# A DiT attention block: turning all four token tiles before the K projection

## The chip, the cores and the metric

The kernel runs on one core of one Trainium2 chip. The metric is the device time of one execution in microseconds (us). The engines are PE (TensorE, with PEld for its weight loads), DVE (VectorE), ACT (ScalarE), POOL (GpSimd) and SP (SyncE, which here only issues transfers).

## What is computed

The reference, cut to the path (x is 2 x 256 x 1152 in bf16, D = 1152; the weights are bf16):

```
mod = (silu(c) @ w_mod).reshape(B, 6, 1, D)
shift_a, scale_a, gate_a = mod[:, 0], mod[:, 1], mod[:, 2]
h = layernorm(x) * (1 + scale_a) + shift_a
q, k, v = split(h @ wqkv, 3)
p = softmax(einsum('bqd,bkd->bqk', q, k) * D ** -0.5)
out = x + gate_a * (einsum('bqk,bkd->bqd', p, v) @ wo)
```

## The kernel before

The 512 tokens (two batches of 256) are four tiles of 128 tokens, t = 0 to 3; tiles 0 and 1 are batch 0. D is nine blocks of 128, k = 0 to 8. Products with weights want the tokens along the free side, so each token tile is centred (its mean taken off, in `xc`), turned block by block on PE (`transposes`, line 249, into PSUM tiles `tp`), copied to `xcT` (line 256), and scaled by 1 + scale_a into `hTs` (lines 309 to 317). The division by the standard deviation is left for later: the deviations are made in `parts_sq` by POOL, turned on PE (`pT3`, line 467), masked, spread over partitions by a matmul with ones (`bc_ps`), and multiplied in afterwards.

**Means.** Tile 0 takes its mean from BN statistics on DVE. Tiles 1 and 2 take theirs from an ACT pass that sums the whole tile (`act_mean`, line 235). Tile 3 is summed by ACT and DVE together, 640 and 512 columns (lines 401 to 405). Variances come later, from `act_var` (ACT) for tiles 1 and 2, and from BN statistics for tile 3.

**Scale.** scale_a = silu(c) @ w_mod is computed in four parts, PA = blocks 0 and 1, PB = 2 to 4, PC = 5 and 6, PD = 7 and 8. For PA, PC and PD the weights are the stationary operand and the result lies along partitions (`scale_rows`, 32 columns a matmul; PA's bank is first filled with ones by `scale_open`, line 273, so its sums already hold the 1). PB uses four 32-column tiles of the array side by side (`scale_tiles`, line 297); its result is turned by DVE (`scale_turned`), which also adds the 1.

**K.** K's transpose is the sum over nine rows k of wK block (k, f) times hTs row k, f = 0 to 8. Five f are accumulated in five PSUM banks (`accs`); the other four are parked: their first two rows go through `psE` banks to `held` in SBUF (`pair`, `pair_part`, `park`, lines 327 to 343), the rest is added later (`held_block`, `add_held`). Rows 0 and 1 are done in three shares of the tokens: batch 0, tile 2, tile 3 (`k_part`, line 322, and the calls at 395 to 425). Tile 3 is summed, centred and turned between them. From row 2 on, a row is one matmul of 512 columns for each f (`k_step`, line 345).

**What sets the order.** Each engine's instructions run in the order in which the code calls them: the recorders (line 76) keep a list for each engine and `pin` (line 98) turns it into dependencies. The profile puts every one of them at line 85, so instructions are told apart by their tiles. Loads run on SP's queue in the order of lines 167 to 192: tiles 0, 1 and 2 of x (tile 2 in two pieces), scale part PA in two pieces, wK row 0, tile 3 of x, wK row 1, scale part PB, wK rows 2 to 4, and so on. PSUM is eight banks: five in a pool MM that goes round, and BA, BB and BC by name. PE starts with eleven filler matmuls on a constant.

Of the kernel before, what the change touches and what calls it, by code (L numbers as in the profile page):

```python
# [7 lines left out]
ACT = mybir.ActivationFunctionType  # L8
ALU = mybir.AluOpType
# [7 lines left out]
def kernel(  # L17
# [10 lines left out]
    P = 128  # L28
# [37 lines left out]
    def bank(shape, name, dtype=None, where=None):  # L66
        if where is None:
            where = ring[turn_no[0] % len(ring)]
            turn_no[0] += 1
        return where[0].tile(shape, dtype or F32, tag=where[1], name=name)  # L70
# [36 lines left out]
    def tok(b):  # L107
        return slice(b * N, (b + 1) * N)

    def one(t):  # L110
        return slice(t * P, (t + 1) * P)
# [22 lines left out]

    c_sb = const.tile([P, B, KT], BF16)
    x_sb = act.tile([P, TT, D], BF16)
    ones_row = const.tile([1, 2 * NR], BF16)
    gps.memset(ones_row, 1.0)
    sca.preload_act_table_set("natural_log_exp_and_others")
    sca.dma_start(out=c_sb, in_=c.rearrange("b (p k) -> p b k", k=KT))  # L140
# [7 lines left out]
    def load_x(t):  # L148
        spq.dma_start(out=x_sb[:, t, :], in_=x_f[t * P : (t + 1) * P, :])
# [4 lines left out]
    def load_s(part, k0, k1):  # L154
        load_mod(wS, 1, k0, k1, part[0] * P, part[1] * P)
# [13 lines left out]
    XS = 104  # L169
    spq.dma_start(out=x_sb[:XS, 2, :], in_=x_f[2 * P : 2 * P + XS, :])  # L170
    spq.dma_start(out=x_sb[XS:, 2, :], in_=x_f[2 * P + XS : 3 * P, :])
    load_s(PA, 0, 4)
    load_s(PA, 4, KT)
    load_k(0, 1)
    load_x(3)
    load_k(1, 2)
    load_s(PB, 0, 4)
    load_s(PB, 4, KT)
# [40 lines left out]
    nmean = const.tile([P, TT], F32)  # L219
    xc = act.tile([P, TT, D], BF16, tag="a1")  # L220
    xcT = act.tile([P, KT, T], BF16, tag="a2")
    ssum3 = small.tile([P, 1], F32, tag="ssum", name="ssum")

    def bn_part(t, st, s):
        vec.bn_stats(out=st[:, s, :], in_=x_sb[:, t, s * CW : (s + 1) * CW])
# [9 lines left out]
    def act_mean(t):  # L235
        sca.activation(out=xc[:, t, :], in_=x_sb[:, t, :], func=ACT.Copy, scale=-1.0 / D,
                       accum_out=nmean[:, t : t + 1])
# [5 lines left out]
    def centre(t, scalar, op, c0=0, c1=D):  # L243
        vec.tensor_scalar(out=xc[:, t, c0:c1], in0=x_sb[:, t, c0:c1], scalar1=scalar, scalar2=None, op0=op)

    HALF = ((0, 4), (4, KT))
    tps = {}

    def transposes(t, h, where):
        k0, k1 = HALF[h]  # L250
        tp = bank([P, 5, P], "tp", BF16, where)
        for k in range(k0, k1):
            ten.transpose(tp[:, k - k0, :], xc[:, t, k * P : (k + 1) * P], ident)
        tps[t, h] = tp

    def xcT_copy(t, h, on_dve, skip=0):
        k0, k1 = HALF[h]
        dst, srct = xcT[:, k0 + skip : k1, one(t)], tps[t, h][:, skip : k1 - k0, :]
        if on_dve:
            vec.tensor_copy(out=dst, in_=srct)  # L260
        else:
            sca.copy(out=dst, in_=srct)

    s1p = const.tile([P, KT, B], F32)
    hTs = act.tile([P, KT, T], BF16, tag="a3")
# [7 lines left out]
    def scale_open(part, where):  # L273
        n = part[1] - part[0]
        psS[part] = bank([P, n, NR], "psS", where=where)
        ten.matmul(psS[part].rearrange("p j r -> p (j r)"), lhsT=junk[0:1, :P], rhs=ones_row[0:1, 0 : n * NR],
                   start=True, stop=False, skip_group_check=True)
# [16 lines left out]
    wS_v = wS.rearrange("p kk (k j c) -> p kk k j c", k=KT, j=4)  # L294
    sT = const.tile([P, KT, 32], F32)

    def scale_tiles(part, where):
        psS[part] = bank([P, part[1] - part[0], 32], "psS", where=where)
        for kk in range(KT):
            for j in range(4):  # L300
                ten.matmul(psS[part][32 * j : 32 * j + 32], lhsT=sc_rhs(kk), rhs=wS_v[:, kk, part[0] : part[1], j, :],
                           start=(kk == 0), stop=(kk == KT - 1))

    def scale_turned(part):
        vec.transpose(out=sT[:, part[0] : part[1], :].rearrange("p k c -> p (k c)"),
                      in_=psS[part].rearrange("p k c -> p (k c)"))
        vec.tensor_scalar_add(out=s1p[:, part[0] : part[1], :], in0=sT[:, part[0] : part[1], 0:B], scalar1=1.0)

    def scaled(k, sl, scalar):
        vec.tensor_scalar(out=hTs[:, k, sl], in0=xcT[:, k, sl], scalar1=scalar, scalar2=None, op0=ALU.mult)  # L310

    def scaled_tp(k, t):
        vec.tensor_scalar(out=hTs[:, k, one(t)], in0=tps[t, 0][:, k, :], scalar1=s1p[:, k, t // NQ : t // NQ + 1],
                          scalar2=None, op0=ALU.mult)

    def scaled_b(k, b):
        scaled(k, tok(b), s1p[:, k, b : b + 1])

    def wk(k, f):
        return wK[:, k, f * P : (f + 1) * P]  # L320

    def k_part(k, sl):
        for f in range(NACC):
            ten.matmul(accs[f][:, sl], lhsT=wk(k, f), rhs=hTs[:, k, sl],
                       start=(k == 0 and sl.start == 0), stop=False, skip_group_check=True)

    def pair(i, b, where):
        return bank([P, 2, N], "psE", where=where), NACC + 2 * i, tok(b)

    def pair_part(pr, k):  # L330
        ps, f0, sl = pr
        for i in range(2):
            ten.matmul(ps[:, i, :], lhsT=wk(k, f0 + i), rhs=hTs[:, k, sl],
                       start=(k == 0 and i == 0), stop=(k == KA - 1), skip_group_check=True)

    def evac(on_dve, out_ap, in_ap):
        if on_dve:
            return vec.tensor_copy(out=out_ap, in_=in_ap)
        return sca.copy(out=out_ap, in_=in_ap)

    def park(pr, on_dve=False):
        ps, f0, sl = pr
        evac(on_dve, held[:, f0 - NACC : f0 - NACC + 2, sl], ps)

    def k_step(k, f0=0, f1=NACC):
        for f in range(f0, f1):
# [13 lines left out]


    fillers(11)
    scale_open(PA, BA)
    sca.activation(out=e_sb, in_=c_sb, func=ACT.Exp, scale=-1.0)
    gps.tensor_scalar_add(out=e_sb, in0=e_sb, scalar1=1.0)
    bn(0, after_second=silu_c)
    centre(0, mvs[:, 0, 0:1], ALU.subtract)
    act_mean(1)
    centre(1, nmean[:, 1:2], ALU.add)
    act_mean(2)  # L370
    gps.tensor_scalar_mul(out=snm[:, 1:3], in0=nmean[:, 1:3], scalar1=float(D) ** -0.5)
    transposes(0, 0, MM)
    transposes(0, 1, MM)
    xcT_copy(0, 0, True)
    xcT_copy(0, 1, False)
    transposes(1, 0, MM)
    transposes(1, 1, MM)
    scale_rows(PA, 0, 4)
    xcT_copy(1, 0, True)
    centre(2, nmean[:, 2:3], ALU.add)  # L380
    xcT_copy(1, 1, False)
    scale_rows(PA, 4, KT, js=[(0, 1), (1, 2)])
    scaled(0, tok(0), psS[PA][:, 0, 0:1])
    vec.tensor_copy(out=s1p[:, PA[0] : PA[1], :], in_=psS[PA][:, :, 0:B])
    transposes(2, 0, BB)
    transposes(2, 1, BC)
    scaled_tp(0, 2)
    scaled_b(1, 0)
    scaled_tp(1, 2)
    xcT_copy(2, 0, True, skip=KA)  # L390
    xcT_copy(2, 1, False)


    accs = [bank([P, T], "acc", where=MM) for _ in range(NACC)]
    k_part(0, tok(0))
    k_part(0, one(2))
    pr20 = pair(1, 0, BA)
    pair_part(pr20, 0)
    pr10 = pair(0, 0, BC)
    pair_part(pr10, 0)  # L400
    H3, C3 = 5 * P, 4 * P
    sca.activation(out=xc[:, 3, 0:H3], in_=x_sb[:, 3, 0:H3], func=ACT.Copy, accum_out=ssum3)
    half3 = small.tile([P, 1], F32, tag="half3", name="half3")
    vec.reduce_sum(out=half3, in_=x_sb[:, 3, H3:D], axis=AX.X)
    vec.tensor_scalar(out=nmean[:, 3:4], in0=half3, scalar1=ssum3, scalar2=-1.0 / D, op0=ALU.add, op1=ALU.mult)
    centre(3, nmean[:, 3:4], ALU.add, 0, C3)
    centre(3, nmean[:, 3:4], ALU.add, C3, D)
    pair_part(pr10, 1)
    k_part(1, tok(0))
    k_part(1, one(2))  # L410
    park(pr10)
    transposes(3, 0, BB)
    pair_part(pr20, 1)
    transposes(3, 1, BC)
    scaled_tp(0, 3)
    scaled_tp(1, 3)
    xcT_copy(3, 0, True, skip=KA)
    park(pr20)
    xcT_copy(3, 1, False)
    st3 = small.tile([P, NCH, 6], F32, tag="stats", name="stats")  # L420
    bn_part(3, st3, 0)
    act_var(1)
    k_part(0, one(3))
    scale_tiles(PB, BB)
    k_part(1, one(3))
    scale_turned(PB)
    for k in range(*PB):
        for b in range(B):
            scaled_b(k, b)
    bn_part(3, st3, 1)  # L430
    bn_part(3, st3, 2)
    vec.bn_aggr(out=mvs[:, 3, :], in_=st3)
    pr11, pr21 = pair(0, 1, BA), pair(1, 1, BC)
    for pr in (pr11, pr21):
        for k in range(KA):
            pair_part(pr, k)
        park(pr, on_dve=(pr is pr21))
    act_var(2)
    parts_sq = const.tile([P, P], BF16)
    gps.memset(parts_sq, 0.0)  # L440
    parts = parts_sq[:, 0 : 3 * TT].rearrange("p (t i) -> p t i", i=3)
# [15 lines left out]
            for b in range(B):  # L457
                scaled_b(k, b)

    for k in range(*PB):  # L460
        k_step(k)
    held_block(0, (2, 4), BA)
    scale_part(PC)
    held_block(0, (4, 5))
    held_block(1, PB, BC)
    pT3 = bank([P, P], "pT3", BF16, BB)
    ten.transpose(pT3, parts_sq, ident)
    masked = const.tile([P, TT, P], BF16)
    vec.tensor_tensor(out=masked, in0=pT3.unsqueeze(1).to_broadcast([P, TT, P]), in1=mask, op=ALU.mult)
    k_step(5)  # L470
    held_block(0, (5, 6))
    held_block(1, (5, 6))
    k_step(6, 0, 2)
# [274 lines left out]
```

## Time and profile before

| what | us |
|---|---|
| median of 3 runs (lowest, highest) | 95.98 (95.83, 96.01) |
| profiled execution | 95.63 |
| its span, first to last instruction | 93.9 |
| PE busy in it | 89.2 |
| DVE, ACT, POOL busy | 69.6, 33.9, 20.8 |
| first transposes of tile 0 on PE | 6.47 |
| first K matmul | 8.95 |
| K's row 2 starts | 14.17 |

The profile is one execution, with times in us from the first instruction. The chain of waits follows the work that ended last back to its start. Times of PE matmuls are pipelined: one starts while the one before still runs, so the distance from start to start is what a matmul costs PE, and its length is when its result is there. A timeline row that stands for several instructions gives the first start and the time to the last end.

### The profile page before, as it was taken

Reading aid. Unit: us, or ns where it says so; the run is one execution under the profiler, and the core shown is the slowest. Engines: PE = TensorE matmul, PEld = TensorE weight load, DVE = VectorE, ACT = ScalarE, POOL = GpSimd, SP = SyncE. Lnnn points to the kernel's source line nnn. Section 1 sums busy time; section 2 is a strip of 40 time slices with the busy share of each in tenths; the row PEclk is TensorE's granted clock in tenths of the full one; section 3 lists DMA queues with packets and bytes.
Section 4 is the critical chain, followed back from the end, with each engine's and each line's share of the span. In section 5 each row is a group of like instructions: output and inputs, shape, how many; then the busy total and the mean of one; then the engine's idle time right before and its main releaser. Section 6 shows DMA issues by size and latency. Waiting matters only on the chain.

```text
span 93.9 us, 1692 instructions
## 1 busy us (share of the span) xinstructions
PE 89.2 (95%) x664; PEld 52.8 (56%) x664; DVE 69.6 (74%) x134; ACT 33.9 (36%) x69; POOL 20.8 (22%) x26
## 2 busy tenths in 40 slices
PE   3999999999999999999999999999999999999970
PEld 1348884545445444444478665656578665665660
DVE  2478789245997977999999899990028587888880
ACT  5188788002643600284220687324246200000010
POOL 5623000800000000000000000008999990002000
PEclk9999999999999999999999999999999999999999
DMA  2999999999999999999999702200000000312212
GB/s 23 345 282 374 372 397 362 369 410 407 407 405 410 414 408 412 402 373 365 381 407 410 296 17 56 63 0 0 0 0 0 0 0 8 125 42 83 114 45 92
DMA packets 17232, 21.31 MB, mean 227 GB/s; under 512 B 2249, under 2 KB 10569, under 8 KB 17225
## 3 DMA queue, kind: packets, MB, share of 16 engines
q1 hardware_dynamic: 16809, 21.17, 62.3%
q8 instruction: 5, 0.08, 0.3%
q10 hardware_dynamic: 416, 0.04, 0.3%
q14 instruction: 2, 0.02, 0.0%
HBM read 19.76 MB, written 1.18 MB: 223 GB/s over the span
## 4 chain that ended last, share of the span: by engine, by line
PE 91%; DVE 4%; issue 1%
PE ps L85 39%; PE psQ L85 19%; PE acc L85 11%; PE psK L85 7%; PE junk_ps L85 5%; PE s_ps L85 4%; PE tp L85 2%; PE psE L85 2%; PE psS L85 2%; DVE o_sb L85 2%; DVE ga L85 2%; PE psH L85 1%; DVE xc L85 1%; DVE junk L85 1%; PE bc_ps L85 0%
## 5 line engine op out<-in xcount | busy, mean ns | idle before, releaser
L85 POOL PARTITION_ALL_REDUCE gate_bc<-gacc x2 | 13.7, 6886 | 44.6 <-DVE gacc L85 44.6
L85 DVE SCALAR_TENSOR_TENSOR gacc<-wG,scT_f,gacc 128x1152 f32<-128x1152 bf16 x16 | 22.4, 1416 | 0.4
L85 PE MATMUL ps<-wV,hT 128*128 128x384 bf16 x108 | 17.7, 326 | 0.0
L85 PE MATMUL psQ<-hT,wQ 128*128 128x512 bf16 x81 | 17.6, 379 | 0.0
L85 PE MATMUL ps<-wO,attnT 128*128 128x384 bf16 (+3 forms) x108 | 17.2, 322 | 0.0
L85 PEld LDWEIGHTS <-attnT 128*128 128x128 bf16 x117 | 11.1, 98 | 6.5
L85 PEld LDWEIGHTS <-hT 128*128 128x128 bf16 x108 | 10.6, 98 | 6.9
L85 PEld LDWEIGHTS <-wK 128*128 128x128 bf16 x109 | 9.5, 97 | 6.9 <-issue 0.2
L85 PEld LDWEIGHTS <-wQ 128*128 128x128 bf16 x81 | 7.9, 98 | 9.6
L85 PE MATMUL acc<-hTs,wK 128*128 128x512 bf16 (+2 forms) x65 | 11.2, 314 | 0.0
L85 DVE TENSOR_TENSOR ga<-ps,gate_bc 128x384 f32<-128x384 f32 (+3 forms) x12 | 6.5, 545 | 3.0 <-PE ps L85 3.0
L85 ACT CAST qkT<-psQ 128x512 bf16<-128x512 f32 x9 | 4.9, 597 | 10.6 <-PE psQ L85 10.6
L85 DVE CAST attnT<-ps 128x512 bf16<-128x512 f32 (+1 forms) x6 | 3.5, 603 | 6.8 <-PE ps L85 6.8
L85 ACT CAST v_sb<-ps 128x384 bf16<-128x384 f32 x12 | 5.5, 476 | 7.9 <-PE ps L85 7.9
L85 PE MATMUL psK<-hTs,wK 128*128 128x512 bf16 x28 | 7.0, 379 | 0.0
L85 DVE TENSOR_TENSOR o_sb<-ga,x_sb 128x384 bf16<-128x384 f32 (+3 forms) x12 | 6.6, 548 | 0.4
L85 ACT CAST o_sb<-ps 128x128 bf16<-128x128 f32 x1 | 0.3, 265 | 17.3 <-PE ps L85 17.3
L85 PE MATMUL junk_ps<-junk 128*128 128x512 bf16 x11 | 4.9, 629 | 1.5 <-DVE junk L85 1.5
L85 DVE TENSOR_TENSOR hT<-hTs,held 128x512 bf16<-128x512 bf16 x9 | 5.8, 688 | 0.4 <-ACT held L85 0.4
L85 DVE BATCH_NORM_STATS2 stats<-x_sb 128x6 f32<-128x384 bf16 x6 | 3.1, 544 | 2.3 <-DMA x_sb<-in_x_dram 2.3
L85 PEld LDWEIGHTS <-junk 128*128 128x128 bf16 (+1 forms) x13 | 1.6, 134 | 5.0 <-issue 3.4
L85 PE MATMUL s_ps<-qkT 128*128 128x256 bf16 x36 | 4.1, 273 | 0.0
(81 smaller groups left out, 84.2 us busy)
## 6 DMA issues: line engine op xcount, KB each, us to landing
wG<-in_w_mod_dram SPq DMA_DIRECT2D x3, 864.0 KB, 12.5
wV<-in_wqkv_dram SPq DMA_DIRECT2D x3, 864.0 KB, 13.4
wO<-in_wo_dram SPq DMA_DIRECT2D x3, 864.0 KB, 9.0
wH<-in_w_mod_dram SPq DMA_DIRECT2D x2, 1152.0 KB, 9.3
wQ<-in_wqkv_dram SPq DMA_DIRECT2D x4, 576.0 KB, 11.7
wK<-in_wqkv_dram SPq DMA_DIRECT2D x7, 288.0 KB, 7.0
wS<-in_w_mod_dram SPq DMA_DIRECT2D x3, 320.0 KB, 6.3
x_sb<-in_x_dram SPq DMA_DIRECT2D x3, 288.0 KB, 3.4
```

The costliest lines, as they stand in the source:

```text
L85: r = fn(*a, **k)
```

## The change

Tile 3 of x is loaded before scale part PA. Tiles 2 and 3 change their way of taking the mean: tile 2 is now summed by ACT and DVE together, tile 3 by ACT alone. All four tiles are centred and turned ahead of K. Blocks 0 and 1 of all tiles go to one PSUM bank (`firsts`, in BA), from which DVE scales them straight into `hTs`, one batch at a time; blocks 2 to 8 of a tile go to one bank (`rests`) and are copied to `xcT` in one piece of 896 columns, three by ACT and the fourth by DVE. K's rows 0 and 1 then run over all 512 tokens (row 0's first two f by batches), and each parked f has a bank and a 512-column matmul for each row. PB's bank is opened with ones like PA's, its nine rounds come in two groups around a park part, and `hTs` takes its scale straight from the turned result. Row 2's first two f run by batches. Row 5 of K goes ahead of the turning of the deviations.

Cut to its core:

```diff
     spq.dma_start(out=x_sb[XS:, 2, :], in_=x_f[2 * P + XS : 3 * P, :])
+    load_x(3)
     load_s(PA, 0, 4)
     load_s(PA, 4, KT)
     load_k(0, 1)
-    load_x(3)
     load_k(1, 2)
...
+    firsts = bank([P, KA, TT, P], "tpA", BF16, BA)
+    def turn_firsts(t):
+        for k in range(KA):
+            ten.transpose(firsts[:, k, t, :], xc[:, t, k * P : (k + 1) * P], ident)
+    def turn_rest(t, where):
+        rests[t] = bank([P, KT - KA, P], "tp", BF16, where)
+        for k in range(KA, KT):
+            ten.transpose(rests[t][:, k - KA, :], xc[:, t, k * P : (k + 1) * P], ident)
+    def copy_rest(t, on_dve=False):
+        evac(on_dve, xcT[:, KA:KT, one(t)], rests[t])
...
+    def scaled_first(k, b, scalar):
+        vec.tensor_scalar(out=hTs[:, k, tok(b)],
+                          in0=firsts[:, k, b * NQ : (b + 1) * NQ].rearrange("p t c -> p (t c)"), scalar1=scalar,
                           scalar2=None, op0=ALU.mult)
...
+    def park_part(i, where):
+        parked[i] = bank([P, T], "psE", where=where)
+        for k in range(KA):
+            ten.matmul(parked[i], lhsT=wk(k, NACC + i), rhs=hTs[:, k, :], start=(k == 0), stop=(k == KA - 1))
...
-    act_mean(2)
+    sca.activation(out=xc[:, 2, 0:SPLIT], in_=x_sb[:, 2, 0:SPLIT], func=ACT.Copy, accum_out=half_a)
+    vec.reduce_sum(out=half_v, in_=x_sb[:, 2, SPLIT:D], axis=AX.X)
+    vec.tensor_scalar(out=nmean[:, 2:3], in0=half_v, scalar1=half_a, scalar2=-1.0 / D, op0=ALU.add, op1=ALU.mult)
+    centre(2, nmean[:, 2:3], ALU.add)
+    act_mean(3)
+    for c0, c1 in ((0, KA * P), (KA * P, D)):
+        centre(3, nmean[:, 3:4], ALU.add, c0, c1)
+    for t, where in ((0, MM), (1, MM)):
+        turn_firsts(t)
+        turn_rest(t, where)
+        copy_rest(t)
     scale_rows(PA, 0, 4)
+    turn_firsts(2)
+    turn_rest(2, BB)
+    copy_rest(2)
+    turn_firsts(3)
+    scale_rows(PA, 4, KT)
+    turn_rest(3, BC)
+    for b in range(B):
+        scaled_first(0, b, psS[PA][:, 0, b : b + 1])
     vec.tensor_copy(out=s1p[:, PA[0] : PA[1], :], in_=psS[PA][:, :, 0:B])
+    for b in range(B):
+        scaled_first(1, b, s1p[:, 1, b : b + 1])
+    copy_rest(3, on_dve=True)
...
+    k_row(0, 2)
+    k_row(1, 0)
     act_var(1)
+    for i in range(NCH):
+        bn_part(3, st3, i)
+    vec.bn_aggr(out=mvs[:, 3, :], in_=st3)
+    park_part(0, BA)
+    park(0)
+    scale_open(PB, BC)
+    scale_tiles(PB, 0, 4)
+    park_part(1, BB)
+    park(1, on_dve=True)
+    scale_tiles(PB, 4, KT)
     scale_turned(PB)
     for k in range(*PB):
         for b in range(B):
-            scaled_b(k, b)
+            scaled(k, tok(b), sT[:, k, b : b + 1])
     act_var(2)
+    park_part(2, BA)
+    park(2)
+    park_part(3, BB)
+    park(3)
...
-    for k in range(*PB):
+    k_row(PB[0], 2)
+    for k in range(PB[0] + 1, PB[1]):
         k_step(k)
...
     held_block(1, PB, BC)
+    k_step(5)
     pT3 = bank([P, P], "pT3", BF16, BB)
...
-    k_step(5)
```

The old calls that these replace (the turning in halves, the pairs, K's shares by tile, the sums and turning of tile 3 between them) go.

More of the change, by code (lines that the diff above doesn't have):

```diff
@@ L136 @@
     x_sb = act.tile([P, TT, D], BF16)
-    ones_row = const.tile([1, 2 * NR], BF16)
+    ones_row = const.tile([1, (PB[1] - PB[0]) * NR], BF16)
     gps.memset(ones_row, 1.0)
@@ L221 @@
     xcT = act.tile([P, KT, T], BF16, tag="a2")
-    ssum3 = small.tile([P, 1], F32, tag="ssum", name="ssum")
     def bn_part(t, st, s):
@@ L244, in centre, with evac @@
         vec.tensor_scalar(out=xc[:, t, c0:c1], in0=x_sb[:, t, c0:c1], scalar1=scalar, scalar2=None, op0=op)
[L246 to L258, printed above, removed]
+    firsts = bank([P, KA, TT, P], "tpA", BF16, BA)
+    rests = {}
+    def turn_firsts(t):
[7 more added lines that the diff above has]
+        evac(on_dve, xcT[:, KA:KT, one(t)], rests[t])
+    def evac(on_dve, out_ap, in_ap):
         if on_dve:
-            vec.tensor_copy(out=dst, in_=srct)
-        else:
-            sca.copy(out=dst, in_=srct)
+            return vec.tensor_copy(out=out_ap, in_=in_ap)
+        return sca.copy(out=out_ap, in_=in_ap)
     s1p = const.tile([P, KT, B], F32)
@@ L295, with scale_tiles @@
     sT = const.tile([P, KT, 32], F32)
-    def scale_tiles(part, where):
-        psS[part] = bank([P, part[1] - part[0], 32], "psS", where=where)
-        for kk in range(KT):
+    def scale_tiles(part, kk0, kk1):
+        for kk in range(kk0, kk1):
             for j in range(4):
                 ten.matmul(psS[part][32 * j : 32 * j + 32], lhsT=sc_rhs(kk), rhs=wS_v[:, kk, part[0] : part[1], j, :],
-                           start=(kk == 0), stop=(kk == KT - 1))
+                           start=False, stop=(kk == KT - 1), skip_group_check=True)
     def scale_turned(part):
@@ L306, in scale_turned @@
                       in_=psS[part].rearrange("p k c -> p (k c)"))
-        vec.tensor_scalar_add(out=s1p[:, part[0] : part[1], :], in0=sT[:, part[0] : part[1], 0:B], scalar1=1.0)
     def scaled(k, sl, scalar):
         vec.tensor_scalar(out=hTs[:, k, sl], in0=xcT[:, k, sl], scalar1=scalar, scalar2=None, op0=ALU.mult)
-    def scaled_tp(k, t):
-        vec.tensor_scalar(out=hTs[:, k, one(t)], in0=tps[t, 0][:, k, :], scalar1=s1p[:, k, t // NQ : t // NQ + 1],
+    def scaled_first(k, b, scalar):
+        vec.tensor_scalar(out=hTs[:, k, tok(b)],
+                          in0=firsts[:, k, b * NQ : (b + 1) * NQ].rearrange("p t c -> p (t c)"), scalar1=scalar,
                           scalar2=None, op0=ALU.mult)
@@ L320, in wk, with k_part, park @@
         return wK[:, k, f * P : (f + 1) * P]
-    def k_part(k, sl):
-        for f in range(NACC):
+    def k_part(k, sl, f0, f1):
+        for f in range(f0, f1):
             ten.matmul(accs[f][:, sl], lhsT=wk(k, f), rhs=hTs[:, k, sl],
                        start=(k == 0 and sl.start == 0), stop=False, skip_group_check=True)
[L327 to L343, printed above, removed]
+    parked = {}
+    def park_part(i, where):
+        parked[i] = bank([P, T], "psE", where=where)
+        for k in range(KA):
+            ten.matmul(parked[i], lhsT=wk(k, NACC + i), rhs=hTs[:, k, :], start=(k == 0), stop=(k == KA - 1))
+    def park(i, on_dve=False):
+        evac(on_dve, held[:, i, :], parked[i])
     def k_step(k, f0=0, f1=NACC):
@@ L362 @@
     fillers(11)
-    scale_open(PA, BA)
+    scale_open(PA, MM)
     sca.activation(out=e_sb, in_=c_sb, func=ACT.Exp, scale=-1.0)
@@ L369 @@
     centre(1, nmean[:, 1:2], ALU.add)
-    act_mean(2)
-    gps.tensor_scalar_mul(out=snm[:, 1:3], in0=nmean[:, 1:3], scalar1=float(D) ** -0.5)
[L372 to L377, printed above, removed]
-    scale_rows(PA, 0, 4)
[L379 to L383, printed above, removed]
@@ L384 @@
-    vec.tensor_copy(out=s1p[:, PA[0] : PA[1], :], in_=psS[PA][:, :, 0:B])
[L385 to L391, printed above, removed]
-    accs = [bank([P, T], "acc", where=MM) for _ in range(NACC)]
[L395 to L419, printed above, removed]
-    st3 = small.tile([P, NCH, 6], F32, tag="stats", name="stats")
[L421 to L425, printed above, removed]
+    SPLIT = 5 * P
+    half_a = small.tile([P, 1], F32, tag="half_a", name="half_a")
+    half_v = small.tile([P, 1], F32, tag="half_v", name="half_v")
+    sca.activation(out=xc[:, 2, 0:SPLIT], in_=x_sb[:, 2, 0:SPLIT], func=ACT.Copy, accum_out=half_a)
@@ new lines, with k_row @@
+    scale_rows(PA, 0, 4)
+    turn_firsts(2)
[6 more added lines that the diff above has]
+        scaled_first(0, b, psS[PA][:, 0, b : b + 1])
+    vec.tensor_copy(out=s1p[:, PA[0] : PA[1], :], in_=psS[PA][:, :, 0:B])
+    for b in range(B):
+        scaled_first(1, b, s1p[:, 1, b : b + 1])
+    copy_rest(3, on_dve=True)
+    accs = [bank([P, T], "acc", where=MM) for _ in range(NACC)]
+    def k_row(k, by_batch):
+        for b in range(B):
+            k_part(k, tok(b), 0, by_batch)
+        k_part(k, slice(0, T), by_batch, NACC)
@@ L426 @@
+    k_row(0, 2)
+    k_row(1, 0)
+    act_var(1)
+    st3 = small.tile([P, NCH, 6], F32, tag="stats", name="stats")
+    for i in range(NCH):
[8 more added lines that the diff above has]
+    scale_tiles(PB, 4, KT)
     scale_turned(PB)
@@ L428 @@
         for b in range(B):
-            scaled_b(k, b)
[L430 to L437, printed above, removed]
+            scaled(k, tok(b), sT[:, k, b : b + 1])
     act_var(2)
+    park_part(2, BA)
+    park(2)
+    park_part(3, BB)
+    park(3)
     parts_sq = const.tile([P, P], BF16)
```

## The prediction

> **What bounds the kernel now.** I read the page's list of engines first, then the chain of waits in order of time, then the timeline of the stretch that the change touches, last the groups of that stretch by shape. The chain is PE for 91% of the span.
>
> ```profile
> PE 89.2 (95%) x664; PEld 52.8 (56%) x664; DVE 69.6 (74%) x134; ACT 33.9 (36%) x69; POOL 20.8 (22%) x26
> ```
>
> ```profile
> 7.59 0.28 issue
> 7.87 0.52 DVE xc L85
> 8.39 0.05 issue
> 8.44 0.68 PE tp L85 x9
> 9.11 0.83 PE acc L85 x10
> ...
> 14.32 3.24 PE acc L85 x15
> ...
> 30.42 17.48 PE psQ L85 x81
> ```
>
> The chain's columns are start, length, what. It leaves PE once between 6.5 and 88 us: at 7.87, where DVE centres x tile 2. From 8.44 on it is PE without a break. So whatever PE loses or wins before 15 us arrives at the end in full, and the sum can stop at a mark: the start of K's fourth row (k = 3). From start to start the trace shows 0.216 us a matmul of 512 columns, 0.109 of 256, 0.056 a transpose or matmul of 128, 0.025 a scale matmul of 32 columns, 0.0425 a round of four tiled scale matmuls (96 columns). Before, row k = 2 starts at 14.17 and the mark is at 14.17 + 5 x 0.216 = **15.25**.
>
> What the present order wastes on PE before the mark can be read off the starts: 0.38 us until 8.44 (tile 2), 0.10 until 11.35 (a bank that ACT empties), 0.04 at 12.11, 0.12 until 12.50 (a bank that DVE empties). These 0.64 us are all the change can take away. A faster stage also has little room below: wH's second part lands at 27.81 and is used from 28.45 (start of psH at 27.95, four rounds of 0.12), so 0.6 us and more of gain would begin to meet transfers.
>
> **The rows that price the new order** (timeline, then groups by shape of 6.2 to 17.4; the groups give busy us, mean ns, idle):
>
> ```profile
> 6.05 0.52 DVE L85 TENSOR_SCALAR xc<-x_sb,nmean 128x1152 bf16<-128x1152 bf16 x1
> 6.35 1.16 ACT L85 ACTIVATE xc<-x_sb 128x1152 bf16<-128x1152 bf16 x1 [0.43 <-DMA x_sb<-in_x_dram]
> 7.42 0.19 ACT L85 ACTIVATION_READ_ACCUMULATOR xc<-x_sb 128x1 f32 x1
> 9.74 0.74 ACT L85 ACTIVATE xc<-x_sb 128x640 bf16<-128x640 bf16 x1
> 10.38 0.19 ACT L85 ACTIVATION_READ_ACCUMULATOR xc<-x_sb 128x1 f32 x1
> ```
>
> ```profile
> L85 ACT COPY xcT<-tp 128x640 bf16<-128x640 bf16 x4 | 2.7, 689 | 0.4 <-PE tp L85 0.4
> L85 DVE TENSOR_SCALAR hTs<-xcT,s1p 128x256 bf16<-128x256 bf16 x7 | 1.5, 282 | 0.0
> L85 DVE TENSOR_SCALAR hTs<-tp,s1p 128x128 bf16<-128x128 bf16 x4 | 1.0, 279 | 0.5 <-PE tp L85 0.5
> L85 DVE COPY xcT<-tp 128x512 bf16<-128x512 bf16 x2 | 0.8, 424 | 0.5 <-PE tp L85 0.5
> L85 DVE TENSOR_REDUCE half<-x_sb 128x1 f32<-128x512 bf16 x1 | 0.7, 673 | 0.0
> L85 DVE COPY held<-psE 128x512 f32<-128x512 f32 x1 | 0.6, 628 | 0.0
> ```
>
> ACT stands idle for x tile 2 until 6.35: that landing starts everything below. A mean of a whole tile is ready 1.26 us after ACT starts on it (6.35 to 7.60), one of 640 columns after 0.83. On DVE the next instruction starts some 0.085 before the last one's end, 0.035 after it if it needs its result; PE starts 0.055 after a DVE result, DVE 0.04 after PE's last end; a matmul's end lies 0.18 (32 columns) to 0.38 (512) behind its start.
>
> **The change, step by step.**
>
> *x tile 3 ahead of the scale weights.* The total of bytes ahead of wK row 0 does not change: its row should land where tile 3 lands now, 9.37 (so far 8.40), and all later loads where they are; the scale parts, now at 6.71 and 7.63, come about 0.8 later. 288 KB behind another costs 0.97 (wK row 0 to tile 3) or 0.78 (tile 3 to wK row 1), so tile 3 lands at 7.13 to 7.32 by these rows, or somewhat before, as large packets fill the time in which the scale's small ones moved only 230 to 340 GB/s. ACT can take it from 7.08. Cost between 0 and 0.24; I take 7.10.
>
> *Tiles 0 and 1* are turned as before, until 7.55; eight scale rows follow, to 7.80 (their weights by 7.5).
>
> *Tile 2.* ACT sums 640 columns to 7.18; DVE, free of the two 512-wide copies, sums the rest to 7.16, makes the mean (0.21) by 7.43 and centres (0.51) by 7.97. PE turns from 8.03 (0.40 earlier than now) to 8.53.
>
> *Tile 3.* ACT's mean at 7.10 + 1.26 = 8.36. Centring costs 0.25 ns a column (512 in 0.353, 1152 in 0.513): 256 columns 0.29, to 8.68; 896 columns 0.45, to 9.05. PE turns the first two blocks at 8.73, issues ten scale rows (last start 9.06, end 9.24), and turns the rest 9.10 to 9.49. DVE can scale only behind the last scale row: 9.28. A 256-wide scaling out of PSUM isn't in the trace: at least 0.28 (128 wide), at most 0.42 (the 512 copy). Half way, 0.35, as the 256 to 512 step of the copies is 0.145; 0.02 more with the scalar in PSUM (0.306 against 0.282). So K starts at 9.28 + 0.37 + 0.055 = **9.70**, now 8.95. Tile 3's nine transposes (0.50) then still lie ahead, so like for like it is 9.70 against 9.45: 0.25 lost.
>
> *K rows 0 and 1.* The work is the same: 2.21 us of K parts become 2.16, sixteen half-wide psE matmuls become eight full ones. The second batch's scaling ends at 9.93, so two half matmuls wait 0.07; row 0 ends at 10.86. DVE goes on to s1p (10.00) and row 1's scalings (10.38, 10.65); row 1 needs them at 10.86 and ends at 11.94. Three accumulators need banks that ACT's 896-wide copies and DVE's s1p empty. A copy costs 0.93 by 0.92 ns a column, within 0.69 and 1.16; they start at 8.27 behind the mean and end at 9.2 and 10.0. PE asks at 10.2 and 10.4: hidden; at 1.16 each 0.1 would show.
>
> *Park parts and scale tiles.* Two full matmuls to 12.37; the bank's opening 0.03 (a new instruction; its 64-wide fellow ran on a cold clock); then the scale tiles in two groups. Going over to 32-column tiles cost 0.09 (psH at 27.95; 0 to 0.12 possible), coming back 0.10 (13.00), so the split adds 0.19. Four rounds, back at 12.77; second park part to 13.20; five rounds, back at 13.60. The third takes it to 14.03. The fourth lies in the bank that DVE's parking of the second empties: psE ends 13.36, the copy takes 0.63, PE goes on at 14.08 and ends at 14.51. BN statistics stand ahead of that parking on DVE, but end at 13.05: no cost. Dropping s1p for PB saves 0.2 of a chain that is late for the other reason.
>
> *Row 2.* Queued behind the parking: the 96-column transpose (13.94 to 14.23), then six scalings. The first serves PE at 14.60 instead of 14.51; four half and three full matmuls end at **15.69**. Against 15.25 that is +0.44.
>
> *k = 5 ahead of the turned rstd.* Now that transpose fills exactly the 0.06 in which row 5's last scaling ends (19.155, PE at 19.209). Moved behind, it leaves the hole and costs its 0.06. Its mask is still ready about 0.2 us before the next scale part needs the bank.
>
> Sum: 0.44 + 0.06 = **+0.50**. The profiled execution took 95.63 (span 93.9 and 1.7 around it); it becomes 96.13. The median of the runs lies 0.35 above that execution, so 95.98 becomes **96.48**. Own range, from the bounds above (PSUM scaling 0.07 either way, tile 3 up to 0.24, switching 0.1): 96.3 to 96.8. About 0.2% (0.19 us) can be told from no change.
>
> **Where a rule speaks against the change.** By the starts, PE's clock rose to full at 6.76 us (fillers 0.43 apart, transposes 0.105 and then 0.056) and held through a stretch of transposes and 32-column matmuls alone, 6.76 to 8.95; the change makes that stretch 0.75 longer, with three holes of about 0.2. The Trainium skill, "TensorE: Matmul & The Clock Gate", Part 1, has the clock halve after an idle window of about 3.4 us, and Part 4 says that transposes don't count as busy in the same way; by that the sum would gain about 1.7 us, an estimate from that page. In this trace the clock held, with K's matmuls from 8.95 on.
>
> **Rivals.**
> - *Tile 2 lands earlier* (no change, 0.21). Now scale packets run on some DMA engines while tile 2's last ones are still out. If it landed at 5.92, where ACT is free, the mean of tile 3 would come 0.43 earlier, K at 9.3 and the mark at about 15.26: 95.85 to 96.17. Against: tile 2 is queued as it was, and nothing new is ahead of it.
> - *PE never waits for a mean* (faster, 0.15). Place: tile 3's mean, forecast at 8.36. With no hole PE would issue from 7.55 eight scale rows, eighteen transposes and ten scale rows, 1.46 us, and start K at 9.01; the waits of 0.07 and 0.14 behind would go with DVE's earlier start, and the mark would come at 14.8, with the 0.06 a gain of 0.4: 95.6. It decides from a mean at 7.86 on, 0.5 earlier than forecast; each 0.1 more is 0.1 of gain. Against: ACT is busy with tile 1 to 5.92 and needs 0.74 + 1.26 from there.
> - *Tile 3 lands late* (slower, 0.06): beyond 7.08 each 0.1 costs 0.1; at 7.7, 97.1.
> - *The clock falls* (slower, 0.03). If PE's rate halved in the longer stretch without K and took as long to come back as it took at the start (1.50 to 6.76), 5.3 us of work would take 2.6 more: 99.1. It decides as soon as transposes and 0.5 us of K no longer hold the clock.
> - *The change does not do what it says*: the changed program's order has tile 3's load as the fifth on SP's queue and all 36 transposes ahead of K, so this gets no chance of its own.
>
> **How the numbers follow.** Forecast 0.55, all of it slower by over 0.2%; with the two slower rivals 0.64. No change 0.21, faster 0.15. The range leaves out the faster case and the clock (0.18): 95.85 to 97.0.
>
> **What would show it.** K's first acc matmul at 9.6 to 9.8 (below 9.4 speaks for the early landing); ACT's mean of tile 3 starting at 7.1 without a DMA wait; DVE's four scalings at about 0.35 each; PE idle for DVE twice, before the fourth park part and before row 2 (14.1, 14.6); the mark at 15.7; psS rounds unchanged at 0.0425. The forecast is wrong if the mark is at or before 15.3, or if time moves behind the mark other than the 0.06.

## The result, and the profile after

The changed kernel takes 96.34 us (median of 13 runs, 96.26 to 97.28) against 95.70 (13 runs, 95.31 to 96.28): **slower, ratio 1.0083, 95% interval 1.0054 to 1.0112**. Its profiled execution took 96.41 (span 94.6; before 95.63 and 93.9).

The page's list of engines and the chain of waits in order of time (start, length, what), as they were shown of the kernel before:

```profile
PE 90.1 (95%) x641; PEld 51.7 (55%) x641; DVE 69.1 (73%) x128; ACT 33.8 (36%) x68; POOL 20.8 (22%) x26
```

```profile
9.28 0.37 DVE hTs L85
9.64 0.04 issue
9.69 2.37 PE acc L85 x12
...
14.82 3.39 PE acc L85 x17
...
31.13 17.48 PE psQ L85 x81
```

PE is still the chain. Between 6.5 and 88 us it leaves PE once, at 9.28, for DVE's scaling ahead of K's first matmul, and Q starts at 31.13 instead of 30.42: 0.71 of the 0.75 us by which the spans differ are there by then. The mark (start of K's row 3) moved from 15.24 to 15.89, 0.65; the turning of the deviations adds 0.06. Between K's first rows and row 2 the timeline shows PE going over to the 32-column tiles twice, the first time by way of the opening (one row):

```profile
11.89 0.59 PE L85 MATMUL psE<-hTs,wK 128*128 128x512 bf16 x2
12.42 0.21 PE L85 MATMUL psS<-ones_row,junk 1*128 1x96 bf16 x1
12.56 0.35 PE L85 MATMUL psS<-wS,scT_rep 128*32 128x96 bf16 x16
12.85 0.60 PE L85 MATMUL psE<-hTs,wK 128*128 128x512 bf16 x2
13.38 0.40 PE L85 MATMUL psS<-wS,scT_rep 128*32 128x96 bf16 x20
13.71 1.11 PE L85 MATMUL psE<-hTs,wK 128*128 128x512 bf16 x4
```

Read the starts, the first column: from 13.71 the four last matmuls, 0.216 apart, would bring row 2 to 13.71 + 4 x 0.216 = 14.57, but it starts at 14.81. The rest is two waits for DVE: 0.08 ahead of the third of these four, whose bank the parking copy empties at 14.18, and 0.15 ahead of row 2, whose first scaling ends at 14.76:

```profile
13.49 0.69 DVE L85 COPY held<-psE 128x512 f32<-128x512 f32 x1 [0.69 <-PE psE L85]
14.10 0.27 DVE L85 STREAM_TRANSPOSE sT<-psS 128x96 f32<-128x96 f32 x1
14.47 1.07 DVE L85 TENSOR_SCALAR hTs<-xcT,sT 128x256 bf16<-128x256 bf16 x5
```

### The profile page after: what moved, and what is told of

It reads as the page before. It is cut to its first block, busy times and chain, and to the rows that moved or that the text cites. A ratio compares the mean times of both kernels' runs of the same rounds, so it can differ in the third digit from the quotient of the medians.

```text
span 94.6 us, 1638 instructions
## 1 busy us (share of the span) xinstructions
PE 90.1 (95%) x641; PEld 51.7 (55%) x641; DVE 69.1 (73%) x128; ACT 33.8 (36%) x68; POOL 20.8 (22%) x26
## 4 chain that ended last, share of the span: by engine, by line
PE 92%; DVE 4%; issue 0%
PE ps L85 38%; PE psQ L85 18%; PE acc L85 11%; PE psK L85 7%; PE junk_ps L85 5%; PE s_ps L85 4%; PE psS L85 2%; PE psE L85 2%; DVE o_sb L85 2%; PE tp L85 2%; DVE ga L85 2%; PE psH L85 1%; PE tpA L85 1%; DVE junk L85 1%; DVE hTs L85 0%
## 5 line engine op out<-in xcount | busy, mean ns | idle before, releaser
L85 PEld LDWEIGHTS <-wK 128*128 128x128 bf16 x85 | 7.8, 97 | 8.6 <-issue 1.1
L85 PE MATMUL acc<-hTs,wK 128*128 128x512 bf16 (+1 forms) x49 | 10.7, 361 | 0.0
```

Of the source, the lines that this page charges most:

```text
L85: r = fn(*a, **k)
```

## The experiments

The theory is the prediction's ledger: PE's order is full, so the loss is the sum of what PE waits for and of the new changes of shape, partly at K's start, mostly between row 1 and row 2. The rivals: the order of loads alone; PE's own work alone; PE's clock. Medians are of 6 to 12 runs beside 17 to 29 runs of the kernel before on the same chip, whose medians were 95.63 to 95.75; a ratio is to those. The changed kernel's own, 96.34, comes from another set, so a difference of medians from it is good to about 0.1. Single executions have no ratio. K's start, and the landings, are from each kernel's one profiled execution.

**One part alone: the load (x1).** In the kernel before:

```diff
+    load_x(3)
     load_s(PA, 0, 4)
     load_s(PA, 4, KT)
     load_k(0, 1)
-    load_x(3)
```

> The kernel before, with one line moved: tile 3 of x is loaded ahead of scale part PA. Theory (the loss comes from what stands behind what on PE and DVE): the second scale piece lands near 8.36 instead of 7.63, PE's ten rows on it wait for it, K's first matmul comes at about 9.2 instead of 8.95 and the rest follows: 0.2 to 0.35 us slower than before. Rival (the order of loads is the whole cause): the full 0.7 us of loss. Rival (the early load is itself a help, since tile 3's sum no longer waits): 0.1 us or more faster.

96.32, ratio 1.0061 (1.0038 to 1.0085). PE in its timeline:

```profile
9.02 0.41 PE L85 MATMUL psS<-scT_rep,wS 128*128 128x32 bf16 x10 [0.83 <-DMA wS<-in_w_mod_dram]
9.29 0.66 PE L85 MATMUL tp<-ident,xc 128*128 128x128 bf16 x9
9.82 0.60 PE L85 MATMUL acc<-hTs,wK 128*128 128x256 bf16 x4
```

The mechanism is the one expected, the size is not: the second scale piece landed at 8.98, not 8.36, and K started at 9.82. wK's row 0 landed at 9.69, so K could not have started at 9.2 whatever the scale piece did; the expectation left this out. The landing of the second scale piece moves from execution to execution: in the ten profiles with the early tile 3 and both pieces of PA it lies between 8.11 and 8.98, in the three with the late one at 7.55 to 7.63. This kernel's own runs spread over 0.9 us (95.76 to 96.66), which would fit, but only one of them has a profile. The size, 0.65, is what the rival asked for that makes the order of loads the whole cause. This run alone doesn't refute it; x2 and x7 (below) do: undoing the early load in the changed kernel makes it slower still, and x7 keeps it and loses nothing.

**The load undone (x2)** in the changed kernel (the reverse of that diff).

> The changed kernel, with only the load of tile 3 put back behind wK row 0. Theory: tile 3 lands at 9.4, ACT's mean of it ends at 10.6, K starts at about 12.0 instead of 9.69, and the time is some 2.2 us over the changed kernel's. Rival (the order of loads is what costs): the time falls to that of the kernel before.

99.58 in one execution, 3.2 over the changed kernel's profiled one, not 2.2. K started at 11.77, 2.1 later, near the 2.3 expected; the other 1.1 has a cause that the windows show (columns: busy us of PE, its weight loads, DVE, ACT, POOL, each with a count, then the granted clock and the DMA share and rate):

```profile
7.40:10.70 3.30, 1.56 (x29) 1.32 (x28) 1.11 (x4) 1.70 (x3) 0.76 (x2) 1.00 1.05 380
10.80:14.10 3.30, 3.30 (x27) 2.18 (x26) 2.94 (x10) 3.11 (x5) 0.00 (x0) 0.50 1.07 392
14.20:17.60 3.40, 3.40 (x49) 1.45 (x48) 1.44 (x4) 1.85 (x4) 0.00 (x0) 1.00 1.13 360
```

PE was busy for under half of one stretch, and then had half its clock for the next, which held K's first matmuls. So the early load is no slip: with all tiles turned ahead of K it is needed, and it has its own price.

**Behind row 1: one group of scale tiles (x3).** In the changed kernel:

```diff
+    park_part(1, BB)
+    park(1, on_dve=True)
     scale_open(PB, BC)
-    scale_tiles(PB, 0, 4)
-    park_part(1, BB)
-    park(1, on_dve=True)
-    scale_tiles(PB, 4, KT)
+    scale_tiles(PB, 0, KT)
```

> The changed kernel, with the second park part ahead of the bank's opening, so PB's nine tiled rounds are one group, and DVE parks sooner. Theory: one change of array shape less (0.19), no wait before the fourth park part (0.08) and less before row 2 (0.15): row 2 starts at 14.35 instead of 14.81, 0.45 us under the changed kernel, 0.2 to 0.35 over the kernel before. Rival (only the array's switching counts): 0.2 us under the changed kernel. Rival (loads or PE's clock are the cause): no change.

95.97, ratio 1.0036 (1.0019 to 1.0053), 0.37 under the changed kernel's median. PE:

```profile
13.00 0.57 PE L85 MATMUL psS<-wS,scT_rep 128*32 128x96 bf16 x36
13.50 1.04 PE L85 MATMUL psE<-hTs,wK 128*128 128x512 bf16 x4
14.38 0.82 PE L85 MATMUL acc<-hTs,wK 128*128 128x256 bf16 x5
```

Row 2 starts at 14.38 instead of 14.81, and without a hole: 13.50 + 4 x 0.216 is 14.36. More than half of the loss is this one place: it takes away a change of shape and both waits for DVE at once, and what each is worth alone this run doesn't show.

**Without the opening of PB's bank (x4)**: the bank starts its sums anew, and `scale_turned` adds the 1 into `s1p`, as before.

> The changed kernel, without the opening of PB's bank: the 1 is added by DVE behind the transpose, as before. PE saves the opening and the change of shape around it, 0.2 us; DVE's chain to row 2 grows by 0.2. Theory (row 2 waits for DVE): within 0.1 us of the changed kernel. Rival (PE's own work is the limit there): 0.2 us under it.

96.47, ratio 1.0088 (1.0062 to 1.0113): the changed kernel's. PE's second group came 0.13 sooner (13.25), and DVE gave it back:

```profile
14.27 0.16 DVE L85 TENSOR_SCALAR s1p<-sT 128x6 f32<-128x6 f32 x1
14.54 0.68 DVE L85 TENSOR_SCALAR hTs<-xcT,s1p 128x256 bf16<-128x256 bf16 x3
```

Row 2 started at 14.88. PE's own work was not the limit there.

**K's start: scale rows ahead of tile 3 (x5).**

```diff
-    turn_firsts(3)
     scale_rows(PA, 4, KT)
+    turn_firsts(3)
```

> The changed kernel, with PA's last ten scale rows ahead of tile 3's first two transposes. Theory (K waits for DVE's scaling, which waits for the last scale row, which PE holds back for tile 3's mean): the rows end 0.1 sooner, K's first matmul comes at 9.60 instead of 9.69 and the time is 0.1 us under the changed kernel. Rival (K waits for the scale weights' landing or for wK): K stays at 9.69.

96.34, ratio 1.0073 (1.0050 to 1.0096): no gain, K at 9.65. Theory and rival were both wrong about the reason. DVE:

```profile
9.24 0.62 DVE L85 TENSOR_SCALAR hTs<-tpA,psS 128x256 bf16<-128x256 bf16 x2 [0.32 <-PE tpA L85]
```

What it waits for is no longer the scale rows but `tpA`, the first blocks of tile 3, which this scaling (batch 0) does not read. They lie in the same bank, one tile of the program. **Two banks (x10)** instead of one on top of this:

```diff
-    firsts = bank([P, KA, TT, P], "tpA", BF16, BA)
+    firsts = {0: bank([P, KA, NQ, P], "tpA", BF16, BA)}
...
+        if t // NQ not in firsts:
+            firsts[t // NQ] = bank([P, KA, NQ, P], "tpA", BF16, MM)
```

> The kernel with PA's last scale rows ahead of tile 3 (x5), with the first blocks of the two batches in two PSUM banks instead of one. There DVE's first scaling waited for tile 3's first transposes, which batch 0 does not need, since they share its bank. Theory: the first scaling starts at the end of the scale rows, 0.1 sooner, and K at 9.55; but a bank more is in use, so an accumulator of row 0 waits for row 1's scalings near 10.6, and row 1 starts no sooner. Rival (the rows' own end, not the bank, holds DVE): K stays at 9.65.

One execution, 96.27. The same row of DVE:

```profile
9.10 0.62 DVE L85 TENSOR_SCALAR hTs<-tpA,psS 128x256 bf16<-128x256 bf16 x2 [0.19 <-PE psS L85]
```

The wait is the scale rows' again, 0.14 sooner, and K starts at 9.50. Row 0's matmul for its fifth f then waits 0.07 (10.48 instead of 10.41), as expected for a bank, and row 2 starts at 14.71 instead of 14.78 in the one-bank version. So with the scale rows first the shared bank holds K back, by 0.15, and freeing it wins little, for eight banks are all there are. In the changed kernel itself the scale rows come last, and its row of DVE (9.28) waits for `psS`.

**Row 5 behind the turning again (x6)** (the diff's last hunk undone).

> The changed kernel, with row 5 of K behind the turning of the deviations again. Theory: the hole of 0.06 ahead of row 5 goes, and from there to the end all is 0.06 sooner. Rival: the turning then waits for POOL's deviations and nothing is won.

96.35 in one execution. From the first held matmul to Q's first it took 12.86 us, before 12.86, in the changed kernel 12.91: the 0.06 is confirmed in the trace, and too small for the times.

**The tail without holes (x7).** On the version without the opening:

```diff
-    scale_tiles(PB, 0, 4)
+    scale_tiles(PB, 0, KT)
     park_part(1, BB)
-    park(1, on_dve=True)
-    scale_tiles(PB, 4, KT)
+    park(1)
...
-    park_part(3, BB)
+    park_part(3, BC)
...
-    k_row(PB[0], 2)
-    for k in range(PB[0] + 1, PB[1]):
+    for k in range(*PB):
...
-    k_step(5)
     pT3 = bank([P, P], "pT3", BF16, BB)
...
+    k_step(5)
```

> The changed kernel up to K's second row; behind it PB's nine rounds in one group right behind the first park part, the 1 added by DVE as before, parking by ACT alone, the fourth park part in the bank that the scale leaves, row 2 undivided, and row 5 behind the turning. Theory: PE runs without a hole from 9.95 on except for the two changes of array shape, row 2 starts at 14.19 and the time is that of the kernel before within 0.1 us, so the whole loss but 0.05 lies behind row 1. Rival (the late start of K is the cause): still 0.25 us or more over the kernel before.

95.78, ratio 1.0007 (0.9983 to 1.0031): the loss is gone, though K starts as late as in the changed kernel. So the late start is paid for by the holes of the old order that the change closes (0.26 behind 8.95, in the prediction's list), and the loss is made behind row 1. Six things differ here from the changed kernel; apart from those that x3, x4 and x6 take alone, their shares aren't separated. The one profile is not of a typical run (95.99): the loads up to wK's row 1 were 0.05 to 0.25 later than in the changed kernel's and PB's first piece 0.6 (K at 9.76), PE stood 0.14 ahead of the fifth of the nine rounds, whose weights come with PB's second piece, and row 2 started at 14.44, not at the expected 14.19:

```profile
12.49 0.71 PE L85 MATMUL psS<-wS,scT_rep 128*32 128x96 bf16 x36
13.13 1.47 PE L85 MATMUL psE<-hTs,wK 128*128 128x512 bf16 x6
```

**And the scale rows ahead of tile 3 (x8)** with it (three f of row 0 by batches):

> The one before, with PA's last scale rows ahead of tile 3 as well, and row 0's first three instead of two f by batches. Theory: K starts at 9.60, no wait in row 0, row 2 at 14.06; 0.1 us under the kernel before. Rival (the earlier start is lost at row 2, which then waits for DVE or weights): no gain over the one before.

95.86, ratio 1.0020 (0.9992 to 1.0049): no gain, the rival's outcome, but not for its reason, for K did not start sooner at all. In its profile wK's row 0 landed at 9.78 and K started at 9.83, though DVE's scaling had ended at 9.57; PB's second piece held PE for 0.22. With the order's own waits gone, the loads are next, in this one profile.

**What holds K's start (x9)?** The changed kernel without the sum of tile 2, which is centred by tile 1's mean:

```diff
-    sca.activation(out=xc[:, 2, 0:SPLIT], in_=x_sb[:, 2, 0:SPLIT], func=ACT.Copy, accum_out=half_a)
-    vec.reduce_sum(out=half_v, in_=x_sb[:, 2, SPLIT:D], axis=AX.X)
-    vec.tensor_scalar(out=nmean[:, 2:3], in0=half_v, scalar1=half_a, scalar2=-1.0 / D, op0=ALU.add, op1=ALU.mult)
-    centre(2, nmean[:, 2:3], ALU.add)
+    centre(2, nmean[:, 1:2], ALU.add)
...
```

> The changed kernel without the sum of x tile 2: it is centred with tile 1's mean, so ACT's and DVE's two part sums and DVE's small step are gone; all else is as changed. Theory (PE's start on K hangs on the chain of sums, tile 2's first): tile 2 is turned from 7.8 to 8.0 on, ACT reaches tile 3 at its landing near 6.7, K starts at 9.35 and the time is 0.3 us under the changed kernel. Rival (the landing of the scale weights or of wK row 0 sets K's start): K stays at 9.6 or later and less than 0.1 us is won.

96.24 (11 runs), ratio 1.0051 (1.0024 to 1.0078): 0.1 under the changed kernel's median, the rival's side. Its profiled execution, left out of these, took 135.72 at a granted clock of 0.67, so PE's times in it are not read, but DVE, ACT and the landings can be:

```profile
7.54 0.19 ACT L85 ACTIVATION_READ_ACCUMULATOR xc<-x_sb 128x1 f32 x1
7.76 0.65 DVE L85 TENSOR_SCALAR xc<-x_sb,nmean 128x256 bf16<-128x256 bf16 x2 [0.77 <-ACT xc L85]
9.25 0.62 DVE L85 TENSOR_SCALAR hTs<-tpA,psS 128x256 bf16<-128x256 bf16 x2 [0.83 <-PE psS L85]
```

Tile 3's mean is there at 7.73, half a microsecond sooner, and DVE's first scaling starts at 9.25 all the same: it waits for scale rows whose weights landed at 8.74. So the sums are not the only bound. **Without the second scale piece's load (x12)** on top of it (rows 4 to 8 use the first piece):

```diff
     load_s(PA, 0, 4)
-    load_s(PA, 4, KT)
...
```

> The kernel without tile 2's sum (x9), and also without the load of the second piece of scale part PA: the scale rows 4 to 8 use the first piece's weights, so 320 KB fewer stand ahead of wK. Theory (two bounds on K's start lie close together: the sums of tiles 2 and 3, and the landings of the scale weights and wK behind the earlier tile 3; x9 took one away and the other held): with both gone K starts at about 9.3 instead of 9.66 and the time is 0.4 us under the changed kernel. Rival (something else on PE, DVE or ACT holds K at 9.6): less than 0.15 us under it.

96.07, ratio 1.0046 (1.0027 to 1.0064): 0.27 under the changed kernel's median, between the theory's 0.4 and the rival's 0.15. In the profiled execution (96.28) K started at 9.63, with wK row 0 landed at 7.95 and tile 3's mean at 7.87:

```profile
7.41 0.33 PE L85 MATMUL tpA<-ident,xc 128*128 128x128 bf16 x2
7.58 0.55 PE L85 MATMUL tp<-ident,xc 128*128 128x128 bf16 x7
7.97 0.35 PE L85 MATMUL psS<-scT_rep,wS 128*128 128x32 bf16 x8
8.17 0.27 PE L85 MATMUL tpA<-ident,xc 128*128 128x128 bf16 x2
```

There is no hole in these starts: here PE itself was the bound, as its transposes ran at half rate (0.107 apart) until 7.51. So three things end within some tenths of each other ahead of K: the sums, the loads, and, where the sums are out of the way, PE's turning when its clock rises late. Taking one or two away shows the next; how much each weighs over many executions is not settled by these runs.

**A hole of the kernel before (x11)**, from the same ledger: DVE's order at tile 2.

```diff
-    xcT_copy(1, 0, True)
     centre(2, nmean[:, 2:3], ALU.add)
+    xcT_copy(1, 0, True)
```

> The kernel before, with one line moved: DVE centres tile 2 ahead of its copy of tile 1's first half. The ledger of the kernel before has its largest hole (0.38) where PE waits for that centring, which DVE starts 0.26 late because of the copy. Theory: centring 7.64 to 8.15, transposes from 8.2, K at 8.77, 0.15 us faster than before. Rival (the first scaling then waits for the copy, or the accumulators for their banks): no change.

95.86, ratio 1.0017 (0.9992 to 1.0042): no change, the rival's outcome. Tile 2 was turned from 8.22 instead of 8.44, but the first scaling needs the copy that was moved, and started at 8.60 instead of 8.29; K stayed at 8.95. No version of these beats the kernel before.

## Why the prediction was right, point by point

The sign, the mechanism and the range held: 96.48 forecast, 96.34 measured, and +0.50 forecast for the sum against +0.71 in the traces (+0.64 between the medians). That the time came within 0.14 is in part luck: the sum was 0.14 to 0.21 too small, and the kernel before, taken at 95.98 from three runs, has a median of 95.70 over 13. The step of 0.35 from the profiled execution to the median was not there (0.07 before, -0.07 after). Steps, forecast and seen, in us:

| step | forecast | trace |
|---|---|---|
| tile 2 turned from | 8.03 | 8.22 |
| ACT's mean of tile 3 | 8.36 | 8.24 |
| tile 3's first blocks from | 8.73 | 8.72 |
| K's first matmul | 9.70 | 9.69 |
| row 1 ends | 11.94 | 11.89 |
| second, third park part | 12.77, 13.60 | 12.85, 13.71 |
| fourth park part | 14.08 | 14.23 |
| row 2 | 14.60 | 14.81 |
| the mark | 15.69 | 15.89 |
| ahead of row 5 | 0.06 | 0.06 |

- *K's start* came to the hundredth by luck, not by the road forecast. Tile 3 landed at 6.71, sooner than the bound from neighbouring loads, and its mean was no longer last. Tile 2 was 0.2 late: DVE's centring ended 0.11 late, and PE, whose clock rose at 7.53 in this execution and not at 6.76, finished tiles 0 and 1 at 7.97 and the scale rows behind them near 8.2. From 8.22 on PE was dense, until DVE's scaling: the forecast hole ahead of tile 3 was not there, and this made up for the late tile 2. The late clock was not needed for it: in x3 and x4 it rose at 4.91 and 5.69, PE stood idle for 0.5 to 0.6 ahead of tile 2, and yet began it at 8.24 and K at 9.70, for PE started 0.15 behind the centring's end (8.09), not the 0.055 of the sum. That DVE's scaling can also wait for tile 3's blocks through the shared bank was not in the working; x10 shows it, 0.15, with the scale rows first.
- *The PSUM scaling* of 256 columns, priced half way between two rows at 0.35, took 0.344 to 0.355.
- *The opening* was mis-sized: with the change to a one-row operand and on to 32-column tiles, from the last park matmul's end at 12.32 to the first round at 12.56, it took 0.24, not 0.12. Yet x4, without it, gained nothing, as DVE was the limit there. The split's change of shape was right (0.09 in, at 13.38; 0.10 out, at 12.85, behind a last round of 0.0425).
- *DVE's tail* was mis-sized by 0.13: the parking copy took 0.69, not the 0.63 of the row before, and the scaling started 0.107 after the transpose, not 0.035. All rows in which DVE waits for its own result and for ACT's have 0.107 (the part mean at 7.31 too); those that wait for its own result alone have 0.035. It is not the number of waits alone: two rows of `o_sb` near the end wait for their own result and a landing, and have 0.034. x3 takes this stretch away and gets 0.43 of start time back; x4 starts DVE's tail 0.13 sooner, lengthens it by the added 1 and gets nothing.
- *The load order* was priced at nothing behind the landing of tile 3. In this arrangement nothing shows a cost, as the sums and PE's turning end as late. Alone it costs 0.6% (x1), and where the rest is mended it is next (x8, one profile).
- *The rivals.* No change and faster did not happen. The late tile 3 did not either. The falling clock did not happen in the changed kernel, but x2 shows that it exists: it came behind a stretch of 3.4 us with PE busy for 1.7 of it.

Three of the changed kernel's 13 runs lie at 97.0 to 97.3. Their granted clock is on record as 1.00, where the halved stretch of x2 made it 0.983, so no such stretch makes them; whether a late landing or a late first rise of the clock does is open, for none of them has a profile.

## What to carry to other kernels

Where PE is dense, a new order is worth only the holes that it closes, less those that it opens: write both ledgers in starts before believing either. Each change of array shape (here about 0.1 us), each wait for a result of one's own and another engine's at once (0.07 more) and each bank shared by an early and a late producer (0.15) is a term of its own. A load that is moved forward moves back what lies behind it; look at who uses those bytes next, and expect its landing to vary (here by 0.9 us). And take the time of the kernel before from as many runs as the forecast needs: three of them were 0.28 off here.

## What the runs showed of the hardware that was not expected

- PE's clock halved for one stretch of 3.41 us (10.75 to 14.16) when the 3.41 before it held only 1.7 us of PE work, all of it transposes and scale rows, in x2. In x4 the stretch from 5.69 to 9.11 held 0.5 us of fillers at its start and then only transposes and scale rows, PE busy 2.4 of 2.9 us, and the full clock stayed. x8 has a cleaner one: 6.25, where its clock rose, to 9.66 held the last 0.13 us of a filler, 36 transposes and 19 scale matmuls, PE busy 3.0 of 3.4 us, and the full clock stayed too. Part 4 of the Trainium skill's "TensorE: Matmul & The Clock Gate" says that transposes don't count as busy in the same way; x4 and x8 speak against this, as far as the scale rows beside them allow. The length of the stretch in x2 is as Part 1 there has it. Where between 1.7 us busy (x2, halved) and 2.4 (x3, 4.91 to 8.32, kept) the line lies these runs don't show.
- The time at which the clock first rose differs from profile to profile, 4.2 (x7, by its fillers' starts: 0.427 apart until 4.03, 0.216 from 4.35) to 7.5 us (the changed kernel), with the same fillers.
- Changing from 128 to 32 columns of the array cost 0.09 us (13.29 to 13.38 in the changed kernel), back 0.10 (12.74 to 12.85), to a one-row operand another 0.10 (12.32 to 12.42).
